# Attention into a mixture of experts on one core: halves of a copied tile, single routing steps, and the order at the experts' entry

## The chip, the core and the metric

The kernel runs on one core of a Trainium2 chip. A core has a matrix engine (TensorE, PE in the profile), a vector engine (VectorE, DVE), a scalar engine (ScalarE, ACT), a general engine (GpSimd, POOL) and a queue engine (SyncE, SP) that issues most transfers. They run their own streams of instructions and wait for each other by semaphores. The metric is device time in microseconds (us) of one launch, lower is better.

## The reference, cut to what matters

```python
# attention: q, k, v of 4 batches x 8 heads x 768 x 64; 4 sink columns, window 128
scores = q @ k.T / sqrt(64)
keep = (column < 4) | (0 <= row - column < 128)
a = softmax(where(keep, scores, -1e9))
x = (a @ v) laid out as 3072 tokens x 512
# experts: 4 groups x 4 experts, one expert per token
g_logits = x @ w_group;          g = argmax;  g_w = softmax(g_logits)[g]
e_logits = x @ w_expert[g];      e = argmax;  e_w = softmax(e_logits)[e]
out[token] = g_w * e_w * (relu(x @ w1[g, e]) @ w2[g, e])     # 512 -> 1024 -> 512
```

## The kernel before

All arithmetic is to fp32 precision. In the experts a weight `rw` from memory is split into a rounded part `whi` (ScalarE) and the rest `wlo = rw - whi` (VectorE), and TensorE multiplies by both. These chunks are converted in one fixed sequence (numbered here from 0; the first four, of 128x512 halves, during attention, the others 128x1024); `wjob` emits the conversions and `prefetch` the loads of raw chunks, on SyncE's queue.

Attention runs over 24 row tiles of 128 rows (6 per batch). The loop `for i in range(NI + 2)` (L1205 on) is a software pipeline: iteration i makes scores, row maxima and exponentials of tile i, transposes and multiplies tile a = i-1 with the values, and finishes tile b = i-2. Within an iteration: `scores`; `evac(a, 0, f)`, the copy of the transposed probabilities out of PSUM into the tile `pw`, half f = 0 by ScalarE and half f = 1 by VectorE; `values(b, 1)`, which multiplies the second head group's `pw` with `vv` on TensorE into `po`; `out_evac(b)`, ScalarE's copy `xT`; `maxima(i, 0)` (VectorE, the custom operation `sm<-ps`, with its result `st`); `sink_t` and `trans` (transposes on TensorE, `tp`); `exps` (ScalarE, `pt<-sm,st`); `natural(b)` (transposes into the token layout) and `logits(b)`; and `norm(b)` (VectorE, `xt`, with the write of the rows to memory). The same tile of PSUM, `tp2` of two banks, takes the transposed halves, bank f for half f; `misc`, where routing keeps its small products, is a part of bank 0 of it.

Routing turns logits into expert numbers, positions and a table. `route_batch` is a generator, one per batch of six tiles; each `yield` ends a unit of one or two small VectorE operations, some of them on GpSimd. A unit that follows `yield "pe"` runs matmuls, one after `yield "rd"` reads their result. `quota[0]` says how many units an iteration may run, from the table `UNITS` (4 to 7) or else `REND` (6). `maxima` calls `unit` between the maxima, which takes one unit off the quota; what is left of the quota at the end of the iteration is run in one burst by `routing(quota[0], (None, "rd"))`. In the order of VectorE that burst lies between `norm`'s `xt` and the next iteration's maxima. The last units of a batch make `bf` and `af` for three tiles at a time (128x384 and 128x336), the operands of the matmul `tt` whose result goes into the table `tab`.

The last two iterations, i = 24 and 25, have no new scores. There the first expert part is begun: each `next(ew)` emits one column block of its first layer (`ph<-un,whi` and `ph<-un,wlo`, four groups of three matmuls on 128x256). When `xt` of the last tiles is in memory, `xg` is gathered from it by an indirect transfer of GpSimd's queue for the rest of that expert. Once the first part is through both layers (`ph`, then `po`), the experts follow one another, and the table and positions of the last batch are made on the way (`tab`, `sel`, `idv`, `key`, `big`, `rank`).

The program is emitted in this order and each engine keeps it (L106 is the helper through which all instructions are recorded, so every row of the profile shows L106). The framework places the semaphore waits.

Of the kernel before, what the change touches and what calls it, by code (L numbers as in the profile page):

```python
# [22 lines left out]
P = 128  # L23
B, H, S, D = 4, 8, 768, 64
NT = S // P
NI = B * NT
# [29 lines left out]
DVELAG = 1.5  # L56
XLEAD = 9
PEGAP = 1.6
REND, TSTEP = 6, 16
UNITS = {7:4,8:7,9:6,10:6,11:6,12:6,13:6,14:6,15:6,16:6,17:6,18:6,19:6,20:6,21:6,22:6,23:6}  # L60
HC = 3
LATE = 6
PELAG = 2.0
# [28 lines left out]
CHOOK = 15  # L92
# [43 lines left out]
def moe_attention(tc, kqT, vN, vS, nsw, wgx, w1, w2, out):  # L136
    nc = Pinned(tc)
    v = nc.vector
    with ExitStack() as top, ExitStack() as att:
# [15 lines left out]
        def const(shape, dt, name):  # L155
            return cp.tile(shape, dt, name=name)
# [18 lines left out]
        tp2 = ps_p.tile([P, 2, 512], F32, name="tp")  # L175
# [176 lines left out]
        def route_batch(i0, nb, lt, wk, pt, tab, na, pick=None):  # L352
            def sm(shape, name, dt=F32):
                return wk.tile([P, MAXB] + shape, dt, name=name, bufs=1)[:, 0:nb]
# [9 lines left out]
            m = row[:, 0:nb * nk].rearrange("p (n k) -> p n k", k=nk)  # L364
# [6 lines left out]
            d = d5[:, :, :, 0:4]  # L371
# [28 lines left out]
            pe = sm([NE], "pe")  # L400
# [26 lines left out]
            s5, m = m, sm([G], "rm")  # L427
# [17 lines left out]
            for j0 in range(0, nb, 3):  # L445
                j1 = min(nb, j0 + 3)
                w = j1 - j0
                v.tensor_tensor(bf[:, j0:j1], colm[:, None, :].to_broadcast([P, w, P]),
                                ga[:, j0:j1, None].to_broadcast([P, w, P]), ALU.is_equal)
                yield 2  # L450
                on.tensor_tensor(af[:, j0:j1], oh[:, j0:j1, :, None].to_broadcast([P, w, NE, na]),
                                av[:, j0:j1, None, :].to_broadcast([P, w, NE, na]), ALU.mult)
                if j1 < nb:
                    yield 2
            yield "pe"
            tt = misc(pt)[:, 0:NE * na]
            for j in range(nb):
# [13 lines left out]
        start = const([P, NE], F32, "start")  # L471
# [190 lines left out]
        state = dict(issued=0, done=0, freed=0, credit=0.0, route=0.0, clk=0.0, at=0.0, dma=0.0, gap=PELAG, dve=0.0)  # L662

        def dve(us):
            state["dve"] = max(state["dve"], state["clk"]) + us
# [128 lines left out]
        def kinds(i):  # L794
            return NBL if i % NT else NBL - 1
# [10 lines left out]
        def evac(i, g, f):  # L806
            e = env[i]
            if f == 0:
                e["pw", g] = wk.tile([P, 12, D], F32, name="pw", bufs=2)
            n = 2 * kinds(i)  # L810
            (v.tensor_copy if f else nc.scalar.copy)(e["pw", g][:, f:2 * n:2], tp2[:, f, 0:n * D].rearrange("p (m q) -> p m q", q=D))

        def sink_copy(i):
            src = env[i]["pt"].rearrange("p m b l x -> p m (b l x)")[:, :, 4 * BW - NSK:4 * BW + NSK]
# [12 lines left out]
        def quarters(g, c, n, lhs, rhs, start=False, stop=False):  # L827
            for l in range(2):
                for j in range(2):
                    d, o = slice(l * D, (l + 1) * D), (2 * g + j) * D  # L830
                    nc.tensor.matmul(po2[j * D:(j + 1) * D, l, g * P + c:g * P + c + n], lhs[d, o:o + D], rhs(d, j),
                                     start=start, stop=stop)
# [9 lines left out]
        def values(i, g):  # L842
            pw = env[i]["pw", g]
            new, old = vts[i], vts.get(i - 1) if i % NT else None
            quarters(g, 0, P, new[:, 0], lambda d, j: pw[d, 2 * j:6 + 2 * j:5], start=g == 0)
            quarters(g, D, D, new[:, 1], lambda d, j: pw[d, 1 + 2 * j], stop=g == 1 and old is None)
            if old is not None:
                quarters(g, 0, P, old[:, 1], lambda d, j: pw[d, 4 + 2 * j:10 + 2 * j:5])
                quarters(g, 0, D, old[:, 0], lambda d, j: pw[d, 8 + 2 * j], stop=g == 1)

        def out_evac(i):
            env[i]["xT"] = xT = wk.tile([P, NDC, P], F32, name="xT", bufs=1)
# [52 lines left out]
                pick = {SNAP: 0, SNAPB: 1, len(BATCHES) - 1: 2}.get(k)  # L905
                rb.append([[(id(lt), x) for x in range(nb)], route(bounds[k], nb, lt, pick), None])

        def routing(k, kinds=(None, "pe", "rd")):
            while k > 0:
                if not rb or not have.issuperset(rb[0][0]):  # L910
                    return False
                kind = rb[0][2] if isinstance(rb[0][2], str) else None
                kind = None if kind == "po" else kind
                if kind not in kinds or (kind == "pe" and state["clk"] < state["at"]):
                    return False
                rb[0][2] = r = next(rb[0][1], "end")
                k -= r if isinstance(r, int) else 1
                if tail:
                    dve(0.6 if kind == "rd" else 0.25)
                state["at"] = max(state["clk"] + state["gap"], state["dve"] + 0.4)  # L920
                if rb[0][2] == "end":
                    rb.pop(0)
            return True
# [261 lines left out]
        def early_work(q):  # L1185
            plan.update(todo=[], at=0, next=0)
            for j in range(q["nt"]):
                xpose(q, j, True)
                yield 0.43
            for k, us in enumerate(layer1_wide(q)):  # L1190
                if k == LATE:
                    wait_for("late")
                    xpose(PARTS[0][1], 0, True)
                yield us

        quota = [0]

        def unit(k):
            if rb and rb[0][2] == "po":
                rb[0][2] = None  # L1200
            elif quota[0] > 0 and routing(1, (None,)):
                quota[0] -= 1

        ew = early_work(PARTS[0][0])
        load_s(0)  # L1205
        for i in range(NI + 2):
            live = i < NI
            quota[0] = UNITS.get(i, REND)
            a, b = i - 1, i - 2
            mid, old = 0 <= a < NI, 0 <= b < NI  # L1210
# [11 lines left out]
            if mid:  # L1222
                evac(a, 0, 0)
                evac(a, 0, 1)
# [9 lines left out]
                warm(FILL[i] if i < len(FILL) else 0, tp2[:, 0, 320:512])  # L1234
            if mid:
                sink_copy(a)
            if not live:
                next(ew)
                if not mid:
                    state["at"] = 0.0  # L1240
                    routing(1, ("pe",))
            if mid:
                if not live:
                    next(ew)
                sink_t(a)
                trans(a, 1)
# [6 lines left out]
            if mid:  # L1253
                evac(a, 1, 0)
# [38 lines left out]
            if live:  # L1293
                exps(i, 1)
                trans(i, 0)
                routing(1, ("rd",))
                unit(4)
                if old:
                    norm(b)
                if later and not gates:  # L1300
                    gather(*later.pop(0))
                if late:
                    late()
                put_gates(2)
                routing(quota[0], (None, "rd"))
            else:
                if mid:
                    next(ew)
                    values(a, 1)
                put_gates(MAXB)  # L1310
                routing(TSTEP, (None, "rd"))
            if old:
                del env[b]
            if i >= CHOOK and (i % 2 or i > NI - 4):
                prefetch(min(RAW, len(raws) + (1 if live else RAW)))
            if not live:
                wjob()
# [296 lines left out]
```

## Time and profile before

| | us |
|---|---|
| median of 3 runs | 507.39 (505.44 to 507.78) |
| profiled execution | 507.18, of which the span 505.4 |
| TensorE busy | 471.8 (93% of the span) |
| VectorE busy | 351.5 (70%) |
| ScalarE busy | 330.1 (65%) |
| mean granted TensorE clock | 0.994 of full speed |

A busy share is an average over stages: attention lasts to about 170 us, the entry of the experts from there to about 215, and the rest is expert work. To see what a stage waits for, one reads its stretch of the table by time, then the waits of the engine that is short of work there, then that engine and its releaser in order of time. An idle time in brackets stands ahead of the instruction that ended it, with the instruction that it waited for last.

### The profile page before, as it was taken

Reading aid. Unit: us, or ns where it says so; the run is one execution under the profiler, and the core shown is the slowest. Engines: PE = TensorE matmul, PEld = TensorE weight load, DVE = VectorE, ACT = ScalarE, POOL = GpSimd, SP = SyncE. Lnnn points to the kernel's source line nnn. Section 1 sums busy time; section 2 is a strip of 40 time slices with the busy share of each in tenths; the row PEclk is TensorE's granted clock in tenths of the full one; section 3 lists DMA queues with packets and bytes.
Section 4 is the critical chain, followed back from the end, with each engine's and each line's share of the span. In section 5 each row is a group of like instructions: output and inputs, shape, how many; then the busy total and the mean of one; then the engine's idle time right before and its main releaser. Section 6 shows DMA issues by size and latency. Waiting matters only on the chain.

```text
span 505.4 us, 15746 instructions
## 1 busy us (share of the span) xinstructions
PE 471.8 (93%) x6025; PEld 399.6 (79%) x6025; DVE 351.5 (70%) x1135; ACT 330.1 (65%) x875; POOL 116.8 (23%) x241
## 2 busy tenths in 40 slices
PE   7999898988869998999999999999999999999994
PEld 5787777767758976898887967888889788877894
DVE  5776886788888678787227425844688888787870
ACT  4888877877968333477237336754778887687861
POOL 3011241214223102324030204220413061204011
PEclk9999999999998999999999999999999999999998
DMA  6456644656754628889424257985988998868200
GB/s 187 142 186 199 199 134 165 196 199 189 218 208 116 246 66 279 271 295 318 162 68 127 78 199 224 378 315 207 327 284 294 396 381 313 293 191 334 65 24 29
DMA packets 49555, 107.47 MB, mean 213 GB/s; under 512 B 8932, under 2 KB 9444, under 8 KB 49472
## 3 DMA queue, kind: packets, MB, share of 16 engines
q1 hardware_dynamic: 45008, 93.17, 54.8%
q0 software_dynamic: 4320, 12.94, 7.2%
q8 instruction: 49, 0.80, 0.7%
q10 hardware_dynamic: 144, 0.28, 0.2%
q14 instruction: 34, 0.28, 0.2%
HBM read 93.58 MB, written 12.93 MB: 211 GB/s over the span
## 4 chain that ended last, share of the span: by engine, by line
PE 58%; DVE 16%; ACT 12%; issue 8%; DMA 2%; POOL 1%; SPq 1%; POOLq 0%; DVEq 0%; ACTq 0%
PE ph L106 26%; PE po L106 25%; ACT pt L106 7%; PE tp L106 5%; DVE pw L106 3%; DVE sm L106 3%; DVE wlo L106 2%; PE ps L106 2%; ACT pw L106 2%; DVE xt L106 1%; ACT whi L106 1%; DVE un L106 1%; DMA ni<-in_nsw 1%; POOL out L106 1%; DMA xg<-xd,gidx 1%
## 5 line engine op out<-in xcount | busy, mean ns | idle before, releaser
L106 DVE TENSOR_TENSOR wlo<-rw,whi 128x1024 fp32r<-128x1024 f32 (+1 forms) x116 | 134.8, 1187 | 30.6 <-ACT whi L106 30.2
L106 PE MATMUL ph<-un,whi 128*128 128x256 f32 (+9 forms) x576 | 128.5, 313 | 0.0
L106 PE MATMUL po<-whi,un 128*128 128x512 f32 (+6 forms) x384 | 126.7, 395 | 0.0
L106 ACT CAST whi<-rw 128x1024 fp32r<-128x1024 f32 (+1 forms) x116 | 114.8, 1019 | 4.7 <-DMA rw<-in_w 2.3
L106 PE MATMUL ph<-un,wlo 128*128 128x160 f32 (+10 forms) x416 | 99.3, 264 | 0.9 <-DVE wlo L106 0.9
L106 PEld LDWEIGHTS ph<-un,whi 128*128 128x128 f32 x576 | 93.7, 189 | 2.4 <-issue 0.6
L106 POOL DMA_INDIRECT out<-ot,sidx x33 | 40.9, 1239 | 224.5 <-ACT ot L106 168.7
L106 ACT ACTIVATE pt<-sm,st 128x204 f32<-128x204 f32 (+1 forms) x192 | 85.6, 451 | 10.9 <-DVE st L106 8.5
L106 PEld LDWEIGHTS po<-whi,un 128*128 128x128 f32 (+5 forms) x384 | 69.7, 183 | 19.9 <-issue 2.1
L106 PE MATMUL po<-wlo,un 128*128 128x512 f32 (+7 forms) x200 | 78.1, 391 | 2.2 <-DVE wlo L106 2.2
L106 PEld LDWEIGHTS ph<-un,wlo 128*128 128x128 f32 x416 | 76.7, 189 | 1.5 <-DVE wlo L106 1.1
L106 DVE CUSTOM_DVE_ANT_0 sm<-ps,msk 128x204 f32<-128x204 f32 (+1 forms) x192 | 56.1, 352 | 0.7 <-DVE msk L106 0.2
L106 POOL DMA_INDIRECT xg<-xd,gidx x33 | 35.6, 1078 | 37.8 <-DVE idz L106 16.2
L106 PEld LDWEIGHTS po<-wlo,un 128*128 128x128 f32 (+6 forms) x200 | 35.7, 178 | 10.6 <-DVE wlo L106 2.6
L106 PE MATMUL ps<-kb,qb 64*64 64x204 f32 (+1 forms) x768 | 41.0, 330 | 3.2 <-DVE lw L106 2.5
L106 PE MATMUL po<-pw,vv 64*64 64x128 f32 (+1 forms) x1408 | 40.3, 251 | 2.8 <-DVE xt L106 2.7
L106 PEld LDWEIGHTS po<-pw,vv 64*64 64x64 f32 x1408 | 35.6, 135 | 7.5 <-DVE xt L106 5.8
L106 DVE COPY pw<-tp 128x384 f32<-128x384 f32 (+1 forms) x48 | 25.6, 533 | 21.7 <-ACT pw L106 21.7
L106 DVE TENSOR_TENSOR hc<-ph,hc 128x160 f32<-128x160 f32 (+6 forms) x64 | 21.4, 336 | 26.7 <-ACT hc L106 26.7
L106 ACT ACTIVATE un<-ph 128x256 fp32r<-128x256 f32 (+1 forms) x40 | 15.3, 384 | 36.1 <-PE ph L106 35.6
L106 ACT ACTIVATION_READ_ACCUMULATOR pt<-sm,st 128x1 f32 x192 | 36.9, 192 | 0.0
L106 ACT ACTIVATE ot<-po,cg 128x512 f32<-128x512 f32 (+7 forms) x25 | 17.0, 680 | 30.4 <-PE po L106 30.4
(199 smaller groups left out, 638.0 us busy)
## 6 DMA issues: line engine op xcount, KB each, us to landing
rw<-in_w SPq DMA_DIRECT2D x128, 512.0 KB, 5.7
kb<-in_kqT SPq DMA_DIRECT2D x23, 272.0 KB, 4.2
qb<-in_kqT SPq DMA_DIRECT2D x24, 256.0 KB, 3.9
vv<-in_vN SPq DMA_DIRECT2D x24, 256.0 KB, 3.2
xd<-xt SPq DMA_DIRECT2D x24, 256.0 KB, 2.4
xg<-xd,gidx POOLq DMA_INDIRECT x33, 6.1
out<-ot,sidx POOLq DMA_INDIRECT x33, 6.1
sv<-in_vS SPq DMA_DIRECT2D x4, 128.0 KB, 3.9
```

The costliest lines, as they stand in the source:

```text
L106: r = f(*a, **k)
```

## The change

Four edits. (1) `evac` writes half 0 to blocks 0 to 5 of `pw` and half 1 to blocks 6 to 11, where the halves were interleaved block by block (a block is 64 columns); `values` reads by the new numbers. (2) `UNITS` is empty and `REND` is 8, so every iteration has a quota of 8; the burst at an iteration's end is replaced by `unit(5)`, one unit, and by at most one step of the new kind "hv", which makes `bf` and `af` for three tiles. (3) In iteration 25 the column blocks of the first expert part are emitted later, and in iteration 24 `values(a, 1)` stands before a column block. (4) `prefetch` is called in every iteration from 15 on.

```diff
-REND, TSTEP = 6, 16
-UNITS = {7:4,8:7,9:6,10:6,11:6,12:6,13:6,14:6,15:6,16:6,17:6,18:6,19:6,20:6,21:6,22:6,23:6}
+REND, TSTEP = 8, 16
+UNITS = {}
...
                 w = j1 - j0
+                yield "hv"
                 v.tensor_tensor(bf[:, j0:j1], colm[:, None, :].to_broadcast([P, w, P]),
                                 ga[:, j0:j1, None].to_broadcast([P, w, P]), ALU.is_equal)
-                yield 2
                 on.tensor_tensor(af[:, j0:j1], oh[:, j0:j1, :, None].to_broadcast([P, w, NE, na]),
                                 av[:, j0:j1, None, :].to_broadcast([P, w, NE, na]), ALU.mult)
-                if j1 < nb:
-                    yield 2
             yield "pe"
...
             n = 2 * kinds(i)
-            (v.tensor_copy if f else nc.scalar.copy)(e["pw", g][:, f:2 * n:2], tp2[:, f, 0:n * D].rearrange("p (m q) -> p m q", q=D))
+            (v.tensor_copy if f else nc.scalar.copy)(e["pw", g][:, 6 * f:6 * f + n], tp2[:, f, 0:n * D].rearrange("p (m q) -> p m q", q=D))
...
-            quarters(g, 0, P, new[:, 0], lambda d, j: pw[d, 2 * j:6 + 2 * j:5], start=g == 0)
+            quarters(g, 0, P, new[:, 0], lambda d, j: pw[d, j:9 + j:8], start=g == 0)
...
-        def routing(k, kinds=(None, "pe", "rd")):
+        def routing(k, kinds=(None, "pe", "rd", "hv")):
...
                 sink_copy(a)
-            if not live:
-                next(ew)
-                if not mid:
-                    state["at"] = 0.0
-                    routing(1, ("pe",))
+            if i == NI + 1:
+                state["at"] = 0.0
+                routing(1, ("pe",))
             if mid:
                 if not live:
+                    next(ew)
                     next(ew)
...
                 put_gates(2)
-                routing(quota[0], (None, "rd"))
+                unit(5)
+                routing(1, ("hv",))
             else:
                 if mid:
+                    values(a, 1)
                     next(ew)
-                    values(a, 1)
                 put_gates(MAXB)
-                routing(TSTEP, (None, "rd"))
+                routing(TSTEP, (None, "rd", "hv"))
             if old:
                 del env[b]
-            if i >= CHOOK and (i % 2 or i > NI - 4):
+            if i >= CHOOK:
                 prefetch(min(RAW, len(raws) + (1 if live else RAW)))
```

What the edits do to the engines' streams is shown at three places. The first is VectorE around iteration 21, from the second `key` to the first of the maxima (`ISA sm,st<-ps`; the row `ISA st` reads its result), with the semaphores that each instruction waits for. Before:

```order
L106 SCALAR_TENSOR_TENSOR key<-oh_196,key 128x16 [waits DVE_49]
L106 TENSOR_REDUCE ktop<-key 128x1 [waits DVE_49]
L106 TENSOR_TENSOR oh_196<-key,ktop 128x16 [waits DVE_49]
L106 TENSOR_TENSOR ktmp<-oh_196,col 128x16 [waits DVE_49]
L106 TENSOR_REDUCE ktop<-ktmp 128x1 [waits DVE_49]
L106 CAST eid_200<-ktop 128x1 [waits DVE_49]
L106 COPY pw<-tp 128x6x64 [waits Activation_49]
L106 TENSOR_REDUCE rs<-oh_3154 128x16
L106 ISA sm,st<-ps_206,msk 128x204 [waits PE_49]
```

And now:

```order
L106 SCALAR_TENSOR_TENSOR key<-oh_196,key 128x16 [waits DVE_49]
L106 COPY pw<-tp 128x384 [waits Activation_49]
L106 TENSOR_REDUCE ktop<-key 128x1 [waits DVE_49]
L106 ISA sm,st<-ps_206,msk 128x204 [waits PE_49]
L106 ISA st 128x1
L106 ISA sm,st<-ps_206,msk 128x204
L106 ISA st 128x1
L106 TENSOR_TENSOR oh_196<-key,ktop 128x16 [waits DVE_49]
```

The copy of the half into `pw` and the first maximum have moved ahead of five small routing steps, which now lie between the maxima; the copy waits for ScalarE's semaphore in both, and has one run of 384 elements where it had 6 of 64.

The second is ScalarE at the entry, from `rdt`, the last exponential of routing, on: `hs` is the first layer's result of the part before its transposition, the two `whi` between are chunks 6 and 7, `un<-tp` takes in the transposed `hs` for the second layer. Before:

```order
L106 ACTIVATE rdt<-rdt 128x30x4
L106 COPY hs<-ph 128x512 x2
L106 CAST whi<-rw 128x1024
L106 ACTIVATE un<-tp 128x4x128 x2
L106 CAST whi<-rw 128x1024
L106 ACTIVATE ot<-po,cg 128x512
L106 CAST whi<-rw 128x1024 x2
```

And now:

```order
L106 ACTIVATE rdt<-rdt 128x30x4
L106 COPY hs<-ph 128x512
L106 CAST whi<-rw 128x1024
L106 COPY hs<-ph 128x512
L106 CAST whi<-rw 128x1024
L106 ACTIVATE un<-tp 128x4x128 x2
L106 ACTIVATE ot<-po,cg 128x512
```

Chunk 6 has moved between the two copies of `hs`, and chunk 7 ahead of `un<-tp`. VectorE's rest of chunk 7, `wlo`, follows: it stood behind the steps `tab` to `rank` and now stands right behind chunk 6, ahead of VectorE's `un<-tp`.

The third is TensorE in iteration 24, from the sink values on (`po<-spT,sv`): `po<-pw,vv` are the values of the second head group, each pair `ph<-un,whi` and `ph<-un,wlo` a quarter of a column block. Before:

```order
L106 MATMUL po<-spT,sv 128x128 x4
L106 MATMUL ph<-un,whi 128x256 x2
L106 MATMUL ph<-un,wlo 128x256
L106 MATMUL ph<-un,whi 128x256 x2
L106 MATMUL ph<-un,wlo 128x256
L106 MATMUL ph<-un,whi 128x256 x2
L106 MATMUL ph<-un,wlo 128x256
L106 MATMUL ph<-un,whi 128x256 x2
L106 MATMUL ph<-un,wlo 128x256
L106 MATMUL po<-pw,vv 64x128 x4
```

And now:

```order
L106 MATMUL po<-spT,sv 128x128 x4
L106 MATMUL po<-pw,vv 64x128 x4
L106 MATMUL po<-pw,vv 64x64 x4
L106 MATMUL po<-pw,vv 64x128 x4
L106 MATMUL po<-pw,vv 64x64 x4
L106 MATMUL ph<-un,whi 128x256 x2
L106 MATMUL ph<-un,wlo 128x256
```

The values come before the column block. Three blocks stood between these sink values and the next transposes `po<-ident,xT` (`natural`), and two stand there now; the third has moved behind `natural` and the logits (`wsd` holds their weights) that follow it.

## Rows read from the trace of the kernel before

**Rows 1.** Table by stretch, whole core: busy time and instructions, granted clock, DMA share, GB/s.

```profile
140.00:160.00 20.00, 16.77 (x412) 14.39 (x412) 16.84 (x83) 15.22 (x57) 6.04 (x19) 0.91 0.53 177
...
240.00:320.00 80.00, 80.00 (x538) 66.64 (x538) 34.96 (x75) 37.37 (x72) 17.17 (x18) 1.00 0.46 153
```

**Rows 2.** The page's costliest groups: VectorE's copies into pw, with the idle time before them.

```profile
L106 DVE COPY pw<-tp 128x384 f32<-128x384 f32 (+1 forms) x48 | 25.6, 533 | 21.7 <-ACT pw L106 21.7
```

**Rows 3.** Waits of TensorE, 55:165: us in total, times, longest.

```profile
PE tp L106 <- DVE pw L106: 5.1, 9, 0.7
PE po L106 <- DVE xt L106: 2.7, 6, 0.7
```

**Rows 4.** ScalarE in order of time: start, duration, operation, idle before it and its releaser.

```profile
67.19 0.47 ACT L106 ACTIVATE pt<-sm,st 128x204 f32<-128x204 f32 x1 [0.25 <-POOL rm L106]
...
106.73 0.47 ACT L106 ACTIVATE pt<-sm,st 128x204 f32<-128x204 f32 x1 [0.60 <-POOL runb L106]
...
140.28 0.47 ACT L106 ACTIVATE pt<-sm,st 128x204 f32<-128x204 f32 x1 [1.00 <-DVE st L106]
...
149.35 0.47 ACT L106 ACTIVATE pt<-sm,st 128x204 f32<-128x204 f32 x1 [1.33 <-POOL runb L106]
```

**Rows 5.** VectorE in order of time, the bursts of iterations 20 and 21.

```profile
138.52 0.28 DVE L106 SCALAR_TENSOR_TENSOR req<-rdt,row 128x120 f32<-128x120 f32 x1 [0.29 <-POOL rdt L106]
...
147.09 0.17 DVE L106 SCALAR_TENSOR_TENSOR key<-oh,key 128x16 f32<-128x16 f32 x1
...
148.19 0.55 DVE L106 COPY pw<-tp 128x384 f32<-128x384 f32 x1
...
148.88 0.36 DVE L106 CUSTOM_DVE_ANT_0 sm<-ps,msk 128x204 f32<-128x204 f32 x1
```

**Rows 6.** Table by stretch around the lowered clock, columns as in rows 1.

```profile
147.00:149.50 2.50, 1.01 (x32) 0.60 (x24) 2.29 (x14) 0.74 (x2) 0.37 (x2) 1.00 0.75 264
149.50:152.00 2.50, 2.46 (x63) 2.35 (x67) 2.47 (x19) 2.50 (x11) 1.15 (x5) 0.82 0.46 166
152.00:154.00 2.00, 2.00 (x34) 1.88 (x28) 1.39 (x5) 2.00 (x9) 0.18 (x1) 0.50 0.00 0
154.00:156.00 2.00, 2.00 (x62) 1.69 (x62) 2.00 (x7) 0.58 (x3) 0.30 (x2) 0.87 0.37 132
```

**Rows 7.** VectorE in order of time: single routing operations of iterations 16 and 17.

```profile
113.87 0.22 DVE L106 RECIPROCAL rss<-row 128x12 f32<-128x12 f32 x1
...
118.45 0.55 DVE L106 TENSOR_TENSOR bf<-colm,row 128x384 fp32r<-128x384 f32 x1
```

**Rows 8.** ScalarE in order of time, the copy of the last row tile.

```profile
171.62 0.58 ACT L106 COPY xT<-po 128x512 f32<-128x512 f32 x1
```

**Rows 9.** TensorE in order of time at the experts' entry.

```profile
172.56 0.77 PE L106 MATMUL ph<-af,bf 128*128 128x112 f32 x6
173.27 0.46 PE L106 MATMUL po<-ident,xT 64*128 64x64 f32 x8
...
180.03 0.63 PE L106 MATMUL ph<-ident,xg 128*128 128x128 f32 x4 [1.25 <-DMA xg<-xd,gidx]
```

**Rows 10.** TensorE's two other waits at the entry, same view.

```profile
196.32 0.50 PE L106 MATMUL po<-wlo,un 128*128 128x512 f32 x1 [2.16 <-DVE wlo L106]
...
211.91 0.39 PE L106 MATMUL ph<-un,wlo 128*128 128x248 f32 x1 [0.89 <-DVE wlo L106]
```

**Rows 11.** ScalarE in order of time, chunks 6 and 7 of the weights.

```profile
188.71 1.05 ACT L106 CAST whi<-rw 128x1024 fp32r<-128x1024 f32 x1
...
191.05 1.05 ACT L106 CAST whi<-rw 128x1024 fp32r<-128x1024 f32 x1
```

**Rows 12.** VectorE in order of time, the same two chunks.

```profile
189.79 1.22 DVE L106 TENSOR_TENSOR wlo<-rw,whi 128x1024 fp32r<-128x1024 f32 x1 [0.40 <-ACT whi L106]
190.94 1.28 DVE L106 SCALAR_TENSOR_TENSOR un<-tp,un 128x512 fp32r<-128x512 f32 x2
...
195.05 1.21 DVE L106 TENSOR_TENSOR wlo<-rw,whi 128x1024 fp32r<-128x1024 f32 x1
```

More of the change, by code (lines that the diff above doesn't have):

```diff
@@ L844, in values @@
             new, old = vts[i], vts.get(i - 1) if i % NT else None
-            quarters(g, 0, P, new[:, 0], lambda d, j: pw[d, 2 * j:6 + 2 * j:5], start=g == 0)
-            quarters(g, D, D, new[:, 1], lambda d, j: pw[d, 1 + 2 * j], stop=g == 1 and old is None)
+            quarters(g, 0, P, new[:, 0], lambda d, j: pw[d, j:9 + j:8], start=g == 0)
+            quarters(g, D, D, new[:, 1], lambda d, j: pw[d, 6 + j], stop=g == 1 and old is None)
             if old is not None:
-                quarters(g, 0, P, old[:, 1], lambda d, j: pw[d, 4 + 2 * j:10 + 2 * j:5])
-                quarters(g, 0, D, old[:, 0], lambda d, j: pw[d, 8 + 2 * j], stop=g == 1)
+                quarters(g, 0, P, old[:, 1], lambda d, j: pw[d, 2 + j:11 + j:8])
+                quarters(g, 0, D, old[:, 0], lambda d, j: pw[d, 4 + j], stop=g == 1)
         def out_evac(i):
```

## The prediction, made before the changed kernel ran

> **What bounds the kernel now.** I read the table by stretch first. From 240 to 320 us TensorE is busy for 80.00 of 80.00 us, so in the expert stage nothing but its own work counts; what the change can gain there is only the time at which that stage begins. In attention it is another picture: from 140 to 160 TensorE has 16.77 of 20, ScalarE 15.22 and VectorE 16.84, the granted clock is 0.91, and no engine is full [rows 1]. Such a stretch is a ring of waits, and one must ask which wait ends last. Of TensorE's waits between 55 and 165 us the largest is that of the transposes (`tp`) for VectorE's copies into `pw`, 5.1 us in 9; that for `xt` is 2.7 us in 6 [rows 3]. Then I looked at ScalarE in order of time, at the first exponential after each `xT`: in the iterations with routing it stands still for 0.25, 0.60, 1.00 and 1.33 us, and the releaser is VectorE's maxima `st` or a small GpSimd step that was finished long before [rows 4]; on VectorE a burst of routing steps stands ahead of those maxima [rows 5]. Last comes the entry of the experts, where TensorE waits 1.25 us for the gather `xg`, 2.16 and 0.89 us for the rest `wlo` of a weight chunk [rows 9, 10]. From there on TensorE has no long wait, so a microsecond won at the entry should be a microsecond at the end.
>
> **Edit 1, two ranges of `pw`.** The copies wait for each other: VectorE stood idle 21.7 us before its 48 copies, all of it put down to ScalarE's copy [rows 2]. If the interleaved writes were the cause, the new ranges would remove it. But in the order of the changed program the copy still waits for ScalarE's semaphore and nothing about that wait has changed (the first place shown above). What the two copies share besides `pw` is the PSUM tile they read. So I take the gain as zero. A write in one run might be quicker than in 6 of 64; I take no gain, since the copy takes 533 ns in the mean [rows 2] for 384 elements, in line with `bf`, which writes 384 elements in one run in 0.55 us [rows 7]. For TensorE's reads the index is only renumbered: zero.
>
> The Trainium skill ("PSUM — Partial Sum Buffer", section "PSUM bank collisions raise a hardware error") says that two engines must be kept apart by bank and quadrant of partitions. By that rule these two copies, one from each bank of `tp2`, would need no order; the trace shows them in order all the same, and the rule would speak for the second rival below.
>
> **Edit 2, the bursts.** In four iterations the small steps leave the path from `xt` to the maxima; what this gives is capped by ScalarE's idle time there.
> - Iteration 9: four steps leave; the stall of 0.25 us goes [rows 4].
> - Iteration 15: six of seven leave; the stall of 0.60 goes [rows 4].
> - Iteration 20: three steps, and VectorE's wait of 0.29 for `rdt` [rows 5], leave, more than 1 us in all; the stall of 1.00 goes [rows 4].
> - Iteration 21: the copy at 148.19 can start where the step behind the second `key` did (147.09 + 0.20 = 147.29), 0.90 earlier, with the first maximum (148.88) as much earlier [rows 5]; of 1.33 go 0.90 and 0.43 stays [rows 4].
>
> Sum 2.75 us. The steps don't vanish: they stand between the maxima now. There ScalarE needs 0.47 us for an exponential and VectorE 0.36 for a maximum [rows 4, 5], and ScalarE has two copies more to make in between, so eight maxima run ahead of eight exponentials by some 0.1 x 8 and the copies' time; 0.8 us of steps fit. I take zero.
>
> Against it: the quota is 8 and one more unit runs after `trans`, so some steps move ahead. In iterations 16, 17, 22 and 23 one unit of about 0.22 us stands newly ahead of `xt`, and in 11, 12, 18 and 23 one `bf` of 0.55 us ahead of the copy [rows 7]. At full price this is 4 x 0.22 + 4 x 0.55 = 3.1 us; at least it is nothing, because VectorE's copy waits anyway, 21.7 / 30 = 0.72 us each time that it does [rows 2], which covers a `bf`. The nearer row is that of the wait: I take 0.7, for the units ahead of `xt` in the main (TensorE waits for `xt` in 6 iterations already, [rows 3]).
>
> The clock: in 147:149.5 TensorE works 1.01 of 2.5 us, and then the granted clock is 0.82, 0.50 and 0.87, so that half of full speed, 1.2 GHz, is the level in the middle [rows 6]. What this takes is 2.5 x 0.18 + 2 x 0.50 + 2 x 0.13 = 1.7 us. The idle stretch ahead of it is that of iteration 21, which I expect 0.90 us shorter. I take 1.0 back, between 0 and 1.7, because a shorter pause may still cost a part.
>
> `tab` moves to a later iteration for two batches, `wlo`'s chunk 0 with it, the other way round: zero.
>
> **Edit 3, the entry.** (a) One column block leaves the place ahead of `natural`. It cannot start at once: `xT` ends at 171.62 + 0.58 = 172.20 [rows 8], and `natural` stood at 173.27 [rows 9], so it comes about 1.0 earlier, and `xt`, its write and the gather `xg` with it. TensorE pays a wait of some 0.4 us: `ph<-af,bf` now begins where the third block did, at about 171.1, and is done at 171.9. Of the wait of 1.25 for `xg` [rows 9] that leaves a gain of 0.85; bounds 0 (gather not earlier) and 1.25.
>
> (b) `wlo` of chunk 7 ran at 195.05, since `whi` ended only at 191.05 + 1.05 = 192.10 and the routing steps were put ahead of it [rows 11, 12]; TensorE waited 2.16 us [rows 10]. Now chunk 6 is split before the second `hs`, chunk 7 takes its slot (188.71 to 189.76), and VectorE does both rests in a row: about 189.4 + 2 x 1.2 = 191.8, against the 194.2 at which TensorE began to wait. The wait goes: 2.16. VectorE's `un<-tp` is up to 1.2 later by that (it was at 190.94, [rows 12]); were all of it on the path, 0.96 would be left, my lower bound.
>
> (c) Of the third wait, 0.89 for chunk 11 [rows 10], the chunks before it are about half a microsecond earlier on VectorE; I take 0.4, between 0 and 0.89.
>
> Sum 3.41 us. Moved past on the queues: `values(a, 1)` only comes earlier (both its copies were long done), and the later column block lies under the wait for the gather.
>
> **Edit 4, loads.** The same chunks are loaded, one per iteration from 16 on. No engine in attention waits for a load of weights there, so zero; if the bursts delayed other loads it would show as a wait for a DMA, of which there is none now.
>
> **Sum.** 2.75 - 0.7 + 1.0 + 0 + 3.41 = 6.46. The profiled execution took 507.18, which lies 0.21 below the median: 507.18 - 6.46 = 500.7, and on the median's footing **500.9**.
>
> **The rivals.** *Only the entry gains.* Attention is a ring, and the time given back there is taken by the next wait: the chain `pe` to `xt` to `po`, with TensorE's 2.7 us for `xt` and 5.1 for the copies unchanged [rows 3]. For it: those waits are in the same iterations as the stalls. Against it: the stalls are on ScalarE, whose work is nearly the whole period. Time 507.39 - 3.41 = 504.0.
>
> *The copies become independent*, by the framework or since the semaphore arrives earlier. TensorE's 9 waits would lose ScalarE's copy, about 0.46 us each, at most 4.1 us; 500.9 - 4.1 = 496.8. Against it: the semaphore in the order.
>
> *VectorE becomes the bound, and it is slower.* It is busy 16.84 of 20 us from 140 to 160 [rows 1]. In eight iterations (8, 9, 14, 15, 16, 20, 21, 22) steps of about 0.6 us are now between the maxima; if VectorE is the last there, all of it delays the exponentials, 4.8 us, the 3.1 us of the moved units are paid in full, and the clock stays down. Then 507.39 - 2.75 + 4.8 + 3.1 - 3.41 = 509.1. It decides from the point where VectorE has no wait left for ScalarE's copy. Against it: those waits of 0.72 us.
>
> *The clock does not come back*: 1.0 more, 501.9, within the forecast's own range.
>
> **How the numbers follow.** The forecast (497.5 to 503) 0.62, only the entry (503 to 505.5) 0.22, independent copies 0.04, slower 0.08; 0.04 remains for no change by causes that I don't see. A measurement can tell about 0.5%, 2.5 us, from no change: faster is below 504.9. So faster 0.80, same 0.12, slower 0.08. The range 497.0 to 506.0 takes in the ends of the clock (1.7 and 0), of the moved units (0 to 3.1), of the entry's three terms, and the case of the entry alone.
>
> **What would show it.** Right: VectorE's idle time before `pw` for ScalarE near 20 us or more; no stall over 0.5 us of the first exponential in iterations 9, 15, 20 and 21; TensorE without its waits for `xg` and the `wlo` of chunk 7; a granted clock of 1.00 from 140 to 165. Wrong: the copies' wait gone; a new wait of exponentials for `st` in the middle of the maxima; a new wait for `un<-tp` or `xg` at the entry; or TensorE's busy share in attention unchanged.

## The result and the profile after

The changed kernel takes 499.38 us in the median of 4 runs (498.5 to 500.06), the kernel before 506.59 in the median of the 4 runs it is compared with; the ratio is 0.9857, 95% interval 0.9823 to 0.989. The profiled execution took 498.5, of which the span is 496.7, against 505.4 before.

The table by stretch of the changed kernel, columns as in [rows 1] (width, then busy time and instructions of TensorE, its weight loads, VectorE, ScalarE and GpSimd, granted clock, DMA share, GB/s):

```profile
140.00:160.00 20.00, 17.22 (x448) 14.14 (x442) 17.95 (x78) 17.01 (x61) 8.14 (x24) 1.00 0.62 197
149.50:152.00 2.50, 2.25 (x68) 1.85 (x72) 2.37 (x7) 1.76 (x8) 0.40 (x2) 1.00 0.09 30
152.00:154.00 2.00, 1.92 (x54) 1.43 (x46) 2.00 (x15) 1.97 (x7) 0.64 (x4) 1.00 0.84 211
240.00:320.00 80.00, 80.00 (x550) 66.14 (x552) 39.47 (x90) 41.72 (x83) 16.01 (x16) 1.00 0.49 167
```

From 140 to 160 us TensorE has 17.22 us where it had 16.77, VectorE 17.95 where it had 16.84, and the granted clock is 1.00 throughout, also where it had been 0.82 and 0.50 [rows 6]. The expert stage is full as before. The page's group of VectorE's copies answers to [rows 2]:

```profile
L106 DVE COPY pw<-tp 128x384 f32<-128x384 f32 (+1 forms) x48 | 25.6, 533 | 20.2 <-ACT pw L106 19.9
```

The same 533 ns for one copy, a mean over two forms of which the 40 copies of 384 elements take 555 ns before and 556 now, and still 19.9 us of idle time for ScalarE's copy: edit 1 has not touched the wait. ScalarE in order of time, at the first exponentials whose stalls had been 1.00 and 1.33 us [rows 4]:

```profile
138.22 0.47 ACT L106 ACTIVATE pt<-sm,st 128x204 f32<-128x204 f32 x1
...
146.14 0.47 ACT L106 ACTIVATE pt<-sm,st 128x204 f32<-128x204 f32 x1 [0.17 <-DVE st L106]
```

The first has no idle time left, the second 0.17. VectorE around the second of these shows why (columns as in [rows 5]): the copy stands behind the second `key`, and one routing step instead of six stands ahead of the maxima.

```profile
145.04 0.17 DVE L106 SCALAR_TENSOR_TENSOR key<-oh,key 128x16 f32<-128x16 f32 x1
145.14 0.55 DVE L106 COPY pw<-tp 128x384 f32<-128x384 f32 x1
145.61 0.16 DVE L106 TENSOR_REDUCE ktop<-key 128x1 f32<-128x16 f32 x1
145.68 0.36 DVE L106 CUSTOM_DVE_ANT_0 sm<-ps,msk 128x204 f32<-128x204 f32 x1
...
146.26 0.17 DVE L106 TENSOR_TENSOR oh<-key,ktop 128x16 f32<-128x16 f32 x1
```

At the entry TensorE in order of time, to be read against [rows 9, 10]:

```profile
168.32 0.46 PE L106 MATMUL po<-ident,xT 64*128 64x64 f32 x8 [0.34 <-ACT xT L106]
...
175.11 0.63 PE L106 MATMUL ph<-ident,xg 128*128 128x128 f32 x4
...
204.33 0.38 PE L106 MATMUL ph<-un,wlo 128*128 128x248 f32 x1 [0.69 <-DVE wlo L106]
```

`natural` pays the small wait that was expected (0.34), the transposes of `xg` have none, and of the two waits for `wlo` only that for chunk 11 is left, 0.69 long. VectorE has the rests of chunks 6 and 7 in one piece, ahead of `un` and of the routing steps up to `rank` (against [rows 12]):

```profile
183.68 2.41 DVE L106 TENSOR_TENSOR wlo<-rw,whi 128x1024 fp32r<-128x1024 f32 x2
186.00 1.28 DVE L106 SCALAR_TENSOR_TENSOR un<-tp,un 128x512 fp32r<-128x512 f32 x2
...
189.78 0.42 DVE L106 TENSOR_REDUCE rank<-big 128x16 f32<-128x256 f32 x1
```

Where the time went is read from the starts of ScalarE's `xT` (row tile of iteration i, in us), the same work in all three profiles. The kernel with edit 3 alone is the second column, since its attention is that of before and its profile shows no lowered clock there.

| start of `xT` in iteration | before | edit 3 alone | changed |
|---|---|---|---|
| 2 | 17.50 | 16.96 | 17.45 |
| 10 | 66.36 | 65.81 | 66.21 |
| 11 | 72.96 | 72.42 | 72.41 |
| 16 | 105.54 | 105.00 | 104.66 |
| 17 | 112.34 | 111.79 | 110.82 |
| 21 | 138.69 | 138.14 | 137.73 |
| 22 | 147.43 | 146.72 | 145.39 |
| 23 | 156.02 | 154.25 | 152.01 |
| 24 | 161.51 | 160.04 | 157.63 |

From iteration 2 to 24 that is 144.01, 143.08 and 140.18 us: attention is 3.83 shorter than in the profile before, 2.90 of it by the order and 0.93 by the clock. Five profiles have the attention order of before: the time from iteration 2 to 24 is 143.08 and 143.27 in the two in which the clock stays up there (edits 3 and 1 alone) and 143.73, 144.01 and 144.06 in the three in which it falls, so the clock's part is 0.5 to 1.0. From there to the transposes of the second `xg` it is 18.52 before and 17.48 after, 1.04 less; from these to the wait for chunk 11, 31.88 and 29.22, 2.66 less. From that point to the last small wait at 378.09 (370.50 after) both take 166.2. That leaves 1.1 us after it, in which the work is the same: over six profiled kernels (before, changed, and each edit alone) this end takes 126.1 to 127.3 us, by no order of the edits, so it is put down to none of them.

The spans of the two profiles differ by 8.7 us, the medians by 7.2. The profiled run of the changed kernel is the fastest of its four (498.5, mean granted clock 0.998); two of the others have a mean granted clock of 0.990 and take 499.94 and 500.06. The profiled run of the kernel before is 0.6 above its median. So the clock's part is read from one execution and is not all in the median.

### The profile page after: what moved, and what is told of

It reads as the page before. It is cut to its first block, busy times and chain, and to the rows that moved or that the text cites. A ratio compares the mean times of both kernels' runs of the same rounds, so it can differ in the third digit from the quotient of the medians.

```text
span 496.7 us, 15747 instructions
## 1 busy us (share of the span) xinstructions
PE 471.2 (95%) x6025; PEld 399.0 (80%) x6025; DVE 350.5 (71%) x1135; ACT 330.0 (66%) x875; POOL 118.8 (24%) x241
## 4 chain that ended last, share of the span: by engine, by line
PE 57%; DVE 18%; ACT 13%; issue 9%; POOL 1%; DMA 1%; POOLq 0%; DVEq 0%; ACTq 0%
PE ph L106 28%; PE po L106 24%; ACT pt L106 8%; PE tp L106 4%; DVE pw L106 3%; DVE sm L106 3%; DVE wlo L106 3%; ACT pw L106 2%; PE ps L106 2%; DVE xt L106 1%; ACT whi L106 1%; DMA ni<-in_nsw 1%; POOL out L106 1%; DVE un L106 1%; ACT spT L106 1%
## 5 line engine op out<-in xcount | busy, mean ns | idle before, releaser
L106 POOL DMA_INDIRECT out<-ot,sidx x33 | 42.1, 1275 | 221.0 <-ACT ot L106 164.4
L106 PEld LDWEIGHTS po<-whi,un 128*128 128x128 f32 (+5 forms) x384 | 69.6, 183 | 19.9 <-issue 2.1
L106 DVE COPY pw<-tp 128x384 f32<-128x384 f32 (+1 forms) x48 | 25.6, 533 | 20.2 <-ACT pw L106 19.9
```

The costliest lines, as they stand in the source:

```text
L106: r = f(*a, **k)
```

## The experiments

All ratios are to the kernel before on the same chip, with their 95% intervals. The kernel before has medians of 506.3 to 508.0 in the groups of runs that these lines come from, so kernels are compared by the ratios first.

| kernel | median us | ratio | interval |
|---|---|---|---|
| changed (all four edits) | 499.38 | 0.9857 | 0.9823 to 0.989 |
| edit 1 alone | 505.79 | 0.9989 | 0.9975 to 1.0004 |
| edit 2 alone | 502.13 | 0.9926 | 0.9902 to 0.995 |
| edit 3 alone | 502.65 | 0.9929 | 0.9904 to 0.9955 |
| edit 4 alone | 506.65 | 1.0014 | 0.9995 to 1.0033 |
| edits 2 and 4 | 502.68 | 0.99 | 0.9868 to 0.9932 |
| edits 2 and 3 | 501.61 | 0.9892 | 0.9863 to 0.9922 |
| changed, PSUM tile split | 489.01 | 0.964 | 0.961 to 0.9669 |
| the same without edit 1 | 489.38 | 0.964 | 0.9607 to 0.9672 |
| before, PSUM tile split | 496.8 | 0.9805 | 0.9764 to 0.9846 |
| changed, split, half the sink copy by VectorE | 495.58 | 0.9769 | 0.9744 to 0.9795 |
| changed, split, `misc` in the second tile | 489.44 | 0.9646 | 0.9617 to 0.9674 |

### Each edit alone

The first four runs put one of the four edits each on the kernel before.

**Edit 1.** The edit is the hunk of `evac` and `values` shown above.

> The kernel before with edit 1 alone (the halves of pw in two ranges). My theory: the wait of VectorE's copy for ScalarE's belongs to the PSUM tile that both read, not to the destination; time within 0.5 us of before, 21.7 us of idle time before the VectorE copies stays above 20, TensorE's wait of tp for DVE pw between 55 and 165 us stays near 5.1. Rival (the interleaved ranges were the cause): the idle time falls below 12 us and the time by some 4 us.

Measured 0.9989, no change that can be told. The page's group:

```profile
L106 DVE COPY pw<-tp 128x384 f32<-128x384 f32 (+1 forms) x48 | 25.6, 533 | 21.4 <-ACT pw L106 21.2
```

21.2 us of idle time against 21.7, and 533 ns per copy in both (555 ns for those of 384 elements, in both). The destination is not the cause, and a write in one run is not faster here.

**Edit 2.** The hunks of `UNITS`, `REND`, the "hv" step and the end of the iteration.

> The kernel before with edit 2 alone (quota 8, no burst, bf and af one per iteration). My theory: attention ends 3.8 us earlier as in the changed kernel; in the order of this kernel the wlo of chunk 7 also stands ahead of tab, so that TensorE's wait of 2.16 us goes too, while the wait of 1.25 for xg stays: 6.0 us less, ratio 0.988. Rival (the gain in attention needs the two ranges or the even loads): under 2.5 us less.

Measured 0.9926, 3.7 us less by the ratio, not 6.0. Attention did more than I expected: `xT` of iteration 24 starts 138.97 us after that of iteration 2 (16.97 to 155.94), 4.1 less than with edit 3 alone and 5.0 less than in the profile before. But the entry gave some back. TensorE:

```profile
162.40 0.39 PE L106 MATMUL ph<-un,wlo 128*128 128x256 f32 x1 [1.91 <-DVE wlo L106]
...
177.12 0.63 PE L106 MATMUL ph<-ident,xg 128*128 128x128 f32 x4 [1.33 <-DVE un L106]
```

A wait of 1.91 for `wlo`, which the kernel before does not have. VectorE makes 8 rests of half chunks (128x512) in the kernel before and 6 here: the fourth chunk, which was converted in two halves, is now converted whole, and right behind attention. Its rest takes 1.38 us. At `xg` the wait has another name, 1.33 for `un`. The wait of 2.16 for chunk 7 is gone here too, without edit 3.

**Edit 3.** The hunks of iterations 24 and 25.

> The kernel before with edit 3 alone (order at the entry). My theory: attention unchanged, the wait for xg gone (1.25, with about 0.3 paid back ahead of natural), the wait for chunk 7 gone (2.16, its wlo stands ahead of tab here too), chunk 11 about 0.2 to 0.4 better: 3.3 us less. Rival (the wait only moves to chunk 11 or un): under 1.5 us less.

Measured 0.9929, 3.6 us less; expected 3.3. TensorE at the entry:

```profile
170.62 0.46 PE L106 MATMUL po<-ident,xT 64*128 64x64 f32 x8 [0.34 <-ACT xT L106]
...
177.39 0.60 PE L106 MATMUL ph<-ident,xg 128*128 128x128 f32 x4
...
207.28 0.38 PE L106 MATMUL ph<-un,wlo 128*128 128x248 f32 x1 [1.38 <-DVE wlo L106]
```

No wait at `xg`, 0.34 paid ahead of `natural`, as expected; the wait for chunk 11 is 1.38, worse than the 0.89 before, where I had expected it to shrink. In this profile the granted clock is 1.00 as long as TensorE works, so against the profile before the clock is a part of the difference; how much of the 3.6 us in the medians it is, these runs do not tell.

**Edit 4.** One line, `if i >= CHOOK:`.

> The kernel before with edit 4 alone (a prefetch in every iteration from 15 on). My theory: nothing waits for those loads; within 0.5 us of before. Rival: the even spread relieves the loads of the tiles of scores and values, 1 us or more less.

Measured 1.0014: alone it is worth nothing, and TensorE's three waits at the entry (1.25, 2.17, 0.89) stand as they were.

### Which edits need each other

The shares of edits 2 and 3 add up to the whole (3.7 + 3.6 = 7.3), although both remove the same 2.16 us. So something must be paid in them that is not paid in the whole, and the 1.91 us of edit 2 alone pointed to the loads.

> Edits 2 and 4 together on the kernel before. My theory: edit 4 alone is worth nothing, but with edit 2 it keeps the conversion of the weight halves inside attention; in edit 2 alone one half slipped to the entry and TensorE waited 1.91 us for wlo at 162.40. Here that wait is gone, attention is as long as in the changed kernel, and the wait of about 1.3 for xg stays: 500.6 us. Rival (loads have no part in it): as with edit 2 alone, 502.1, with the same wait for wlo.

The wait of 1.91 is gone, as my theory had it: `xT` of iteration 24 starts 140.30 us after that of iteration 2, 1.3 later than with edit 2 alone, since the conversion is back in attention (8 rests of half chunks again). That price I had left out of the expected time. The waits at the entry and behind it:

```profile
176.01 0.63 PE L106 MATMUL ph<-ident,xg 128*128 128x128 f32 x4 [1.34 <-DVE un L106]
...
214.52 0.50 PE L106 MATMUL ph<-un,whi 128*128 128x248 f32 x2 [1.68 <-DVE un L106]
```

The wait of 1.34 ahead of `xg` stays. That of 1.68 is in neither of the edits alone; the second profile of the kernel before has one of its kind once (1.23 at 221.55), the first has none, so I lay it to no edit. The time does not decide: 0.99, with 499.5 to 505.1 us for the eight runs, and an interval (0.9868 to 0.9932) that holds both the 0.989 of my theory and the 0.992 of the rival. The rows speak for my theory. The other pair tells more:

> The changed kernel without edits 1 and 4, that is edits 2 and 3 alone. My theory after the last runs: edits 1 and 4 carry nothing, 499.4 within 0.8. Rival (the even loads carry part of it when the entry is reordered, a half of a weight chunk slips to the entry as with edit 2 alone): 501 or more, with TensorE waiting for wlo near 162 us.

Here the rival was right: 501.6 (0.9892), some 2 us above the changed kernel (the two intervals still overlap), and the rows say why. VectorE makes two rests in one piece right after attention. The row has the form of the first, a half (0.68 us); the second is not a half, as I had expected, but the whole fourth chunk (128x1024, 1.38 us), and TensorE waits for it:

```profile
160.77 1.98 DVE L106 TENSOR_TENSOR wlo<-rw,whi 128x512 fp32r<-128x512 f32 x2
```

```profile
162.80 0.39 PE L106 MATMUL ph<-un,wlo 128*128 128x256 f32 x1 [1.91 <-DVE wlo L106]
```

The table by stretch behind that wait, columns as above:

```profile
160.00:162.00 2.00, 0.79 (x5) 0.38 (x3) 2.00 (x4) 0.33 (x1) 0.99 (x2) 1.00 0.82 299
162.00:164.00 2.00, 1.20 (x25) 1.07 (x29) 1.11 (x3) 0.39 (x1) 1.10 (x2) 0.81 0.94 243
164.00:166.00 2.00, 2.00 (x32) 1.66 (x29) 0.53 (x2) 0.00 (x0) 0.00 (x0) 0.50 0.97 336
166.00:168.00 2.00, 2.00 (x40) 1.93 (x35) 0.00 (x0) 0.00 (x0) 0.00 (x0) 0.84 1.07 419
```

TensorE works 0.79 and 1.20 of 2 us, then the granted clock is 0.50 for the stretch 164 to 166, which is 1.2 GHz. So edit 4 carries about 2 us of the whole, as far as two ratios with overlapping intervals can tell: not by loads that come sooner for their own sake, but since `wjob` emits no conversion before the program's own plan counts the load as landed. With the earlier loads the fourth chunk is converted in halves under attention; without them it is left for the entry, and there, once edit 3 has taken the other waits away, TensorE waits for it. Attention itself is 0.80 longer for it (140.18 against 139.38 from iteration 2 to 24).

### What makes the two copies wait

The reading of the order was that the wait comes from the PSUM tile that both engines read. The edit on the changed kernel:

```diff
-        tp2 = ps_p.tile([P, 2, 512], F32, name="tp")
+        tps = [ps_p.tile([P, 512], F32, name=f"tp{f}") for f in range(2)]
...
-            (v.tensor_copy if f else nc.scalar.copy)(e["pw", g][:, 6 * f:6 * f + n], tp2[:, f, 0:n * D].rearrange("p (m q) -> p m q", q=D))
+            (v.tensor_copy if f else nc.scalar.copy)(e["pw", g][:, 6 * f:6 * f + n], tps[f][:, 0:n * D].rearrange("p (m q) -> p m q", q=D))
...
-            nc.scalar.copy(spT.rearrange("p (f q) -> p f q", f=2), tp2[:, :, 6 * D:7 * D])
+            for f in range(2):
+                nc.scalar.copy(spT[:, f * D:(f + 1) * D], tps[f][:, 6 * D:7 * D])
```

The lines left out only put the new names in; `misc` stays with the first tile. The last hunk is the sink copy, ScalarE's copy `spT` of the transposed sink columns, which read both banks at once and is now made in two halves.

> The changed kernel with the PSUM tile of the transposes split in two, one per bank, and the sink copy in two halves, both by ScalarE. My theory: VectorE's copy waits for ScalarE's because both read one PSUM tile. Here the copies of the first head group lose the wait, those of the second wait for the shorter sink copy: idle time of DVE pw for ACT under 12 us (20 in the changed kernel), but ScalarE has 24 more copies of about 0.15 us; time between 496.5 and 499.5. Rival (the wait comes from elsewhere): idle time near 20 and time 1 us or more above the changed kernel.

489.0 us, 0.964: 10.4 below the changed kernel, where I had allowed 2.9 at most, and had expected the wait to stay for the copies of the second head group. Of this 8.9 us lie between the `xT` of iterations 2 and 24 (131.28 against 140.18). In the changed kernel VectorE's largest wait between 45 and 155 us was this (us in total, times, longest):

```profile
DVE pw L106 <- ACT pw L106: 10.6, 16, 1.1
```

All of VectorE's waits between 45 and 155 us now:

```profile
DVE pe L106 <- PE tp L106: 4.4, 3, 1.5
DVE tab L106 <- PE tp L106: 4.2, 2, 2.3
DVE xt L106 <- PE po L106: 2.6, 5, 0.8
DVE sm L106 <- ACT pt L106: 0.9, 3, 0.5
DVE wlo L106 <- ACT whi L106: 0.5, 1, 0.5
DVE un L106 <- ACT un L106: 0.4, 1, 0.4
```

The wait of `pw` for ScalarE's copy is not in the list any more. ScalarE and VectorE in order of time, in one place:

```profile
42.88 0.41 DVE L106 COPY pw<-tp 128x256 f32<-128x256 f32 x1
42.95 0.36 ACT L106 COPY pw<-tp 128x256 f32<-128x256 f32 x1
```

The two copies of one step run side by side, 42.88 to 43.29 and 42.95 to 43.31, out of the two banks. The Trainium skill ("PSUM — Partial Sum Buffer", section "PSUM bank collisions raise a hardware error") has engines kept apart by bank and quadrant of partitions. This case agrees: copies out of two banks run at once, and the wider order, by tile, had cost 10.4 us. No run splits the sink copy without the tile, so what that half of the edit does by itself is not shown.

The same kernel without edit 1, the halves interleaved in `pw` again:

> The changed kernel with the split PSUM tile, but without edit 1: the halves are interleaved in pw again. My theory: the destination has no part in the wait; as with the split and the ranges, 489.0 within 0.7, no idle time of VectorE's copies for ScalarE's copy. Rival (with the PSUM tile split, the interleaved ranges order the copies): the wait is back and the time is 495 or more.

489.4 and the same ratio, 0.964. Between 45 and 155 us VectorE has no wait for ScalarE's `pw` here either (one of 1.1 us for `spT`). So the destination does not order the copies even where they are free to run together, and edit 1 is not half of a cure either.

On the kernel before, the split alone:

> The kernel before, unchanged but for the split PSUM tile. My theory: the freed copies and the spread routing steps work on different waits, so the split gives as much here as in the changed kernel, about 10 us: 496.5. Rival (the bursts stand in the way, the freed time is lost at the first exponentials): 501 or more.

496.8, 0.9805, about 10 us less as expected. TensorE's old waits at the entry are all there:

```profile
168.20 0.63 PE L106 MATMUL ph<-ident,xg 128*128 128x128 f32 x4 [1.23 <-DMA xg<-xd,gidx]
...
184.49 0.50 PE L106 MATMUL po<-wlo,un 128*128 128x512 f32 x1 [2.16 <-DVE wlo L106]
...
200.11 0.38 PE L106 MATMUL ph<-un,wlo 128*128 128x248 f32 x1 [0.89 <-DVE wlo L106]
```

The two causes are independent within the noise: 0.9805 x 0.9857 = 0.9665, and both together gave 0.964 (0.961 to 0.9669).

### Can more be had from the split

In the split kernel ScalarE makes two sink copies where it made one. In the first try VectorE takes the second of them, and `misc` goes to the second tile, so that no tile is read by both:

```diff
-                nc.scalar.copy(spT[:, f * D:(f + 1) * D], tps[f][:, 6 * D:7 * D])
+                (v.tensor_copy if f else nc.scalar.copy)(spT[:, f * D:(f + 1) * D], tps[f][:, 6 * D:7 * D])
...
-                return spare() if tail else tps[0][:, 384:512]
+                return spare() if tail else tps[1][:, 384:512]
```

> As tpsplit, but the second half of the sink copy by VectorE and the small products of routing in the second bank, so that no VectorE read shares a PSUM tile with a ScalarE read of the same step. My theory: no wait of VectorE's copies for ScalarE's is left; TensorE's waits of 5.2 us for them between 50 and 160 us fall below 2 and the time to about 496. Rival (VectorE, with 24 more copies of about 0.15 us, is the bound): 499.5 or more.

495.6: the number came as forecast (496), but by luck. The copies' wait is gone, as I had said, but it is gone in the split before too, and against that this kernel is 6.6 us slower. TensorE's wait for VectorE's copies, which was to fall below 2 us, is 3.7 between 50 and 160 us. Of the 6.6 us 3.4 lie between the `xT` of iterations 2 and 24 (134.63 us against 131.28) and 2.4 ahead of them (18.97 against 16.56); there TensorE works 0.70 us from 14 to 16, where it works 1.56 in the split, and the granted clock is then 0.54 and 0.60 from 16 to 20 us. VectorE in order of time:

```profile
38.03 0.23 DVE L106 COPY spT<-tp 128x64 f32<-128x64 f32 x1 [0.58 <-PE tp L106]
...
43.15 0.22 DVE L106 COPY spT<-tp 128x64 f32<-128x64 f32 x1 [0.72 <-PE tp L106]
```

The sink copy stands in VectorE's order between the maxima and waits there for TensorE, 0.58 and 0.72 us, and the maxima behind it wait with it; ScalarE's wait of `xT` for TensorE is 17.7 us in the whole span, 7.3 in the split before. VectorE's load has hardly changed (94.5 us busy of the 110 from 45 to 155, 93.8 in the split), so I read the place of the copy in its order as the cause; no run has the copy in another place. With `misc` alone in the second tile (the last line of the diff above):

> As tpsplit, with routing's small products in the second bank, the one that VectorE reads. My theory: ScalarE's copies no longer wait for VectorE's pe, cnt and tab (0.9 us in all in tpsplit): 488.3. Rival (those products now wait for VectorE's copy of the second bank): 489.5 or more.

489.4, the same as the split within its interval. TensorE's waits for `pw` between 45 and 155 us:

```profile
PE tp L106 <- DVE pw L106: 2.4, 6, 1.0
```

That is the rival's new wait (in the split kernel the same wait is 0.2 us). It is not all: behind one of 1.00 us at 113.61 this profile has the granted clock at 0.50 from 116 to 122 us. Up to the `xT` of iteration 19 it is 1.4 us quicker than the split from iteration 2 on (95.85 against 97.27), and the next iteration is 2.3 longer (9.97 against 7.72). How much of what was saved goes in the wait and how much in the clock is not shown; the run with a mean granted clock of 0.997 took 488.96, the other three, at 0.989 and 0.990, 489.4 to 489.6. The best kernel of the study is the changed one with the split tile, 489.0 us.

### The lowered clock

> The kernel before, unchanged, a second profile. My theory: a low granted clock follows one of the two long pauses of TensorE (after 147 us, or the 2.16 us before 196), not always the same one: the profile of before had it at 150 to 156, that of edit 1 alone, with the same order, at 196 to 200, that of edit 3 alone nowhere. Rival (it belongs to the iteration 21 alone): low from 150 to 156 again.

The second profile of the kernel before has it at 150 to 156 again (0.77, 0.50, 0.93), and so has edit 4 alone. Edit 1 alone, whose instructions have the same order, has it elsewhere, behind the wait for chunk 7 (2.17 us in this profile):

```profile
196.00:198.00 2.00, 2.00 (x6) 1.52 (x5) 1.79 (x11) 1.44 (x2) 0.47 (x1) 0.54 1.05 409
198.00:200.00 2.00, 2.00 (x7) 1.62 (x6) 1.83 (x11) 1.13 (x2) 0.56 (x1) 0.60 1.03 303
```

Edit 3 alone, with the attention of before, has it nowhere as long as TensorE works. So this run speaks for the rival, and the profiles taken together against it: the pause of iteration 21 often leads to it and need not. Where it falls is not settled here.

## Why the prediction was right

The forecast was 500.9 and the time 499.4; the direction and the size were right, 7.2 us less against 6.5. Step by step:

- **Edit 1 at zero**: right, and for the reason given (0.9989; 21.2 us of idle time). The rule of the Trainium skill that I set against it ("PSUM — Partial Sum Buffer", section "PSUM bank collisions raise a hardware error") fits the hardware of this case, as the split shows; the order here was wider than that rule asks. One reading was loose: 533 ns is the mean over copies of 384 and 256 elements, those of 384 take 555, which is closer still to the 0.55 us of `bf`.
- **The bursts, 2.75**: right in each of the four places, though the first gave more than its stall. Between the `xT` of iterations 10 and 11, 16 and 17, 21 and 22, 22 and 23, the changed kernel is 0.41, 0.63, 0.92 and 0.91 us shorter than the profile with edit 3 alone, 2.87 in all, where 0.25, 0.60, 1.00 and 0.90 were expected. That the steps cost nothing between the maxima is right too: no exponential waits for them by more than 0.17 in those places.
- **Moved units, -0.7**: mis-sized. From iteration 2 to 24 the order gives 2.90 in all, so the moved units, with the moved table steps, cost nothing on balance (2.87 - 2.90). Taking the nearer bound, the wait that covers them, would have been enough. The balance hides two exchanges that I had put at zero: the two iterations that lose `tab` are 1.88 and 2.10 us shorter than with edit 3 alone (11 to 12, 18 to 19), the two that take it on 1.65 and 2.67 longer (13 to 14, 19 to 20), 0.34 more in all; other iterations make up for that.
- **The clock, +1.0**: 0.93 in attention by the profile before, 0.5 to 1.0 over five profiles. That it comes back holds for the profiled run; two of the four runs of the changed kernel have a lower mean granted clock (0.990) than the profile of before (0.994), so in the median the term stays unshown. And the premise, that it belongs to iteration 21, is weaker than I had it: the profile of edit 1 alone had it at the entry, 1.5 us dear there (17.13 us from the wait for chunk 7 to that for chunk 11, against 15.59 before), and that of edit 3 alone not at all.
- **Entry (a), 0.85**: 1.04 measured, with the wait of 0.34 that was expected to be paid.
- **Entry (b), 2.16, and (c), 0.4**: together 2.66 measured against 2.56. Of the second only 0.20 came (0.89 to 0.69). What was wrong is the edit I laid (b) to: edit 2 alone removes that wait as well, and edit 3 alone too.
- **Edit 4 at zero**: the step that failed. I looked for an engine that waits for a load and found none, and called it free. Alone that is so (1.0014). In the whole it is worth about 2 us by the medians, since no conversion is emitted before the plan counts its load as landed: the cover to name was the place of the conversion, not the wait for the load. The error did not show in the sum, since the order that I read was that of all four edits together, with the conversion inside attention.
- **Rivals.** "Only the entry gains" is out: attention gained 2.90. "VectorE becomes the bound" is out: its waits for ScalarE's copy are still 19.9 us. "The copies become independent" didn't happen, but its price, 4.1 us, was wrong by more than half: made to happen, it gave 10.4. I had counted only TensorE's waits that the profile puts down to VectorE's copy, 9 times 0.46. But the wait holds up what stands behind it in VectorE's order too, and that shows under other names: between 45 and 155 us TensorE's wait for `lw` (VectorE's copy of the logits) falls from 2.6 to 0.5 with the split, and ScalarE's wait of `xT` put down to the maxima `st`, 5.8 us in the changed kernel, is not in the list any more. Neither row that I had gives the 10.4: 4.1 is under half of it, and VectorE's 21.7 us of idle time is twice it.

## What to carry to other kernels

When two engines copy halves of one PSUM tile, look at the semaphores of the built program before blaming the destination: a tile for each bank let the copies run together and was worth more (10 us) than the whole change. Small steps that an in-order engine must do anyway belong behind the work that others wait for, a step or two at a time; a step that itself waits for another engine doesn't belong there (3.4 us of attention were lost with one 0.2 us copy per iteration, `misc` having moved too). An edit that is worth nothing alone may hold up another: take edits away from the whole as well as adding them one by one.

## What the runs showed of the hardware

Copies by ScalarE and VectorE out of different banks of PSUM run at the same time and take about as long as in turn: for 384 elements 473 and 551 ns in the mean in the split kernel, 466 and 555 before. VectorE's copy of 384 elements takes 555 ns in the mean as 6 of 64 (before) and 556 as one run (changed). The granted clock fell to half of full speed, the lower of its two levels, behind pauses of TensorE: 0.98 of 2.5 us busy in the second profile of before, 0.79 of 2 with edits 2 and 3, 0.70 of 2 and 0.98 of 2 in the last two variants of the split kernel. It stayed down for some 4 us, in one profile (`misc` in the second tile) for some 7. And it did not fall behind each such pause: in the profile of before TensorE works 0.16 us from 194 to 196 and with edit 2 alone 0.49 from 160 to 162, and the granted clock is 1.00 there and in the stretches that follow.
